# The last block of a fused attention and MoE kernel: one store per bank from two queues, and each bank copied by two engines

## The chip, the core and the metric

The kernel runs on one core of a Trainium2 chip. Its time is the device time of one execution in microseconds (us). The core has a matrix engine (TensorE, PE in the profile), a vector engine (VectorE, DVE), an activation engine (ScalarE, ACT), GpSimd (POOL) and a sync engine (SyncE, SP) that mostly issues transfers. Data are moved between device memory and the core's SBUF by 16 DMA engines; matrix products leave TensorE into eight banks of 128 partitions by 512 fp32 numbers (PSUM), from which ScalarE or VectorE copies them to SBUF.

## The reference

```python
batch, n_heads, seq, head_dim = (8, 8, 576, 64)
n_tokens, d_model, d_ff = (4608, 512, 2048)
...
out_d = sm_attn(q_d, k_d, v_d)          # on means of 4 tokens
out_up = np.repeat(out_d, factor, axis=2)
...
out_local = np.matmul(attn, v)          # band |i-j| < 4
return (out_up + out_local).astype(np.float32)
...
h = x @ w_in
P = a[0] + a[1] * h + a[2] * h2 + a[3] * h3
Q = 1.0 + np.abs(b[0]) * np.abs(h) + np.abs(b[1]) * h2
g = P / (Q + 1e-06)
return (g @ w_out).astype(np.float32)
```

The sum of a pooled and a local attention is the input x (4608 tokens by 512) of a two-layer network with a rational function between its layers. The result is 4608 rows of 512 fp32 numbers, 2 KB each, 9.44 MB in all.

## The kernel before, in words

Tokens go through the network in nine blocks of 512 (`block_plan`, L57). Block b of the first eight holds the first 512 tokens of batch b (`FULL`, L39). The ninth holds what is left, 64 tokens (`REST`) from each of the eight batches, so its output rows lie in eight pieces of the result, each 64 rows long, with 576 rows from the start of one to the start of the next. For the ninth block `blk.b` is None.

Each block takes 16 steps, one for each 128 of the 2048 hidden features (`steps`, L863). A step has a first-layer part (`h_part`, L899, matmul at L923), the rational function on ScalarE and VectorE (`middle`, L938) and a second-layer part (`o_part`, L974, matmul at L989). The second-layer part trails by two steps and adds into four banks, `ob[0]` to `ob[3]`, one for each 128 tokens of the block. After the last step `store(k)` (L1001) copies the four banks to SBUF and stores them.

The order on every engine comes from a planner (`Plan.run`, L118): each piece of work is put in with `add(engine, cost, function, reads, writes, due)`, and the planner starts what is ready by due time. What it returns is the order of issue; the waits between engines are then derived by the framework from what each instruction reads and writes.

In `store` the first eight blocks copy each bank with one ScalarE copy (L1012) and store it with one transfer of 128 rows from SP's queue (L1020). In the ninth, banks 0 and 2 are copied by ScalarE and banks 1 and 3 by VectorE (L1010), and each bank leaves in two transfers of 64 rows, since its 128 partitions hold the tails of two batches. These are eight transfers of 64 rows by 512 columns, all from SP. After them stands the end of the program: SP waits for every transfer's semaphore (L1247).

Of the kernel before, what the change touches and what calls it, by code (L numbers as in the profile page):

```python
# [17 lines left out]
B, H, S, D = 8, 8, 576, 64  # L18
NT = B * S
DM, DF = 512, 2048  # L20
P = 128
# [17 lines left out]
FULL = 512  # L39
# [17 lines left out]
def block_plan():  # L57
    plan = [Block([(b, 0, FULL)]) for b in range(B)]
    return plan + [Block([(b, FULL, REST) for b in range(B)])]
# [14 lines left out]
class Plan:  # L74
# [11 lines left out]
    def add(self, engine, dur, fn, reads=(), writes=(), due=None, lag=None, load=0.0, after=0.0):  # L86
        t = Task()
        t.engine, t.dur, t.fn, t.due, t.n = engine, dur, fn, due, len(self.tasks)
        t.load, t.after = load, after
        t.lag, t.preds, t.succs, t.late, t.start = lag, {}, [], 1e9, None  # L90
        rk = set().union(*(r.keys for r in reads)) if reads else set()
        wk = set().union(*(w.keys for w in writes)) if writes else set()
        t.uses = {k[1]: k in wk for k in rk | wk if k[0] == "P"}
        for k in rk | wk:
            w = self.writer.get(k)
            if w is not None:
                t.preds[w] = True
        for k in wk:
            for r in self.readers.get(k, ()):
                t.preds.setdefault(r, False)  # L100
            self.writer[k] = t
            self.readers[k] = []
        for k in rk - wk:
            self.readers[k].append(t) if k in self.readers else self.readers.__setitem__(k, [t])
        t.preds.pop(t, None)
        for p in t.preds:
            p.succs.append(t)
        self.tasks.append(t)
        return t
# [78 lines left out]
def attention_moe(  # L188
# [12 lines left out]
    nc = tc.nc  # L201
# [3 lines left out]
    add = plan.add  # L205
# [5 lines left out]
    def put(name, shape, dtype, at=None):  # L211
        nonlocal top
        offset = top if at is None else at
        n = 2 if dtype == BF16 else 4
        for d in shape[1:]:
            n *= d
        if at is None:
            top = -(-(offset + n) // 32) * 32
        ap = nc.alloc_sbuf_tensor_at(name, shape, dtype, offset=offset).ap()
        room = Room(ap, (("S", k) for k in range(offset // 32, -(-(offset + n) // 32))))  # L220
        room.at = offset
        room.size = n
        return room

    def part(room, ap, lo, n):

        r = Room(ap, (("S", k) for k in range((room.at + lo) // 32, -(-(room.at + lo + n) // 32))))
        r.at, r.size = room.at + lo, n
        return r

    def flat(t):
        return t.rearrange("p a b -> p (a b)")
# [5 lines left out]
    for name, parts in (("wl", low2), ("wh", high2)):  # L238
        for w in range(2):
            for f in range(0, NFC, 2):  # L240
                t = put(f"{name}{w}_{f}", [P, 2, NCC, P], F32R)
# [9 lines left out]
    xs, xsf = [], []  # L251
# [604 lines left out]
    blocks = block_plan()  # L856
# [9 lines left out]
    def due_h(n):  # L866
        m = blocks[0].nstep
        return H0 + H_FIRST * min(n, m) + H_STEP * max(0, n - m)
# [132 lines left out]
    def store(k):  # L1001
        blk = blocks[k]
        due = due_h(blk.first + blk.nstep + 2)
        for sub in range(blk.nsub):
            po = ob[sub]
            hi, osb = blk.x[0], xsf[blk.slot][0]
            room = part(hi, None, 4 * sub * DM, 4 * DM)
            osb = flat(osb.ap)[:, sub * DM : (sub + 1) * DM]
            if k == len(blocks) - 1 and sub % 2:
                add("DVE", 0.6, lambda osb=osb, po=po: nc.vector.tensor_copy(out=osb, in_=po.ap), (po,), (room,), due=due)  # L1010
            else:
                add("ACT", 0.49, lambda osb=osb, po=po: nc.scalar.copy(out=osb, in_=po.ap), (po,), (room,), due=due)  # L1012
            if blk.b is not None:
                rows = [(blk.b, sub * P, P)]
            else:
                rows = blk.rows[2 * sub : 2 * sub + 2]
            for i, (b, t, n) in enumerate(rows):
                add(
                    "SP", 0.7,
                    lambda osb=osb, b=b, t=t, n=n, i=i: nc.sync.dma_start(  # L1020
                        out=out[b * S + t : b * S + t + n, :], in_=osb[i * n : (i + 1) * n, :]
                    ),
                    (room,), (), due=due + 2,
                )


    order = sorted(((w, f) for w in range(2) for f in range(0, NFC, 2)), key=lambda c: c[1] / 2 + 1.5 * c[0])
# [69 lines left out]
    for n in range(NS + LAG):  # L1097
        if n < NS:
            k, s = steps[n]
            for f in range(blocks[k].fg):  # L1100
                h_part(n, f)
                if n < NAT:
                    if n % 2:
                        parts(0, n - 1, due_h(n - 1 + blocks[0].nstep) - 2.0)
                    if n == NAT - 1 and NAT < blocks[0].nstep:
                        split_x(0, due_h(NAT) - 3.0)
            if s == blocks[k].nstep - 1:

                if k + 1 < len(blocks):
                    split_x(k + 1)  # L1110
        o = n - LAG
        if o >= 0:
            k, s = steps[o]
            for f in range(blocks[k].fg):
                o_part(o, f)
            if s == blocks[k].nstep - 1:
                store(k)
                if blocks[k].b is not None and blocks[k].b + 2 < B:
                    attend(blocks[k].b + 2)

        if n < NS:
            middle(n)
# [21 lines left out]
    for t in pe:  # L1144
        at = idle_bank(t)
        n = int(WARM * (t.start - max(end, at[0])) / 0.107) if at else 0
# [105 lines left out]
```

## Time and profile before

| What | Value |
|---|---|
| median of 3 runs | 961.99 us (961.51 to 962.8) |
| the profiled execution | 961.83 us |
| its span, first to last instruction | 960.0 us |
| mean granted TensorE clock | 0.996 |
| TensorE busy | 939.1 us, 98% |
| VectorE / ScalarE busy | 843.4 us, 88% / 812.4 us, 85% |
| moved by the DMA engines | 89.26 MB |

The profile is of one execution. A row of the timeline reads: start and duration in us, engine, line, operation, output and input, shapes, number of instructions merged; in brackets what the engine waited for. SPq stands for instructions on SP that issue transfers. In the view of the DMA, a packet is one row of a transfer (or one write to a semaphore of 4 bytes, counted under 512 B), and a queue's share is the time that its packets took, of the time of all 16 DMA engines in the window.

### The profile page before, as it was taken

The page shows a single profiled execution, that of the slowest core. Times are in us where ns is not written, and L with a number is a line of the kernel's source. Part 1 is how long each engine was busy: PE and PEld are TensorE (multiplying, and loading weights), DVE is VectorE, ACT ScalarE, POOL GpSimd, SP SyncE. Part 2 cuts the span into 40 slices and gives each one's busy share as a digit, 9 for nine tenths or more (in the row PEclk, how much of TensorE's full clock was granted, in tenths as well). Part 3 has the DMA queues.
Part 4 walks back from the last instruction along what each step waited for, and adds up shares of the span by engine and source line. Part 5 has one row for each costly group of instructions (what it writes and reads, how often), then busy time and mean ns, then how long its engine had stood idle before and what let it go on. Part 6 is the DMA issues. An engine that isn't in the chain of part 4 may idle for free.

```text
span 960.0 us, 19318 instructions
## 1 busy us (share of the span) xinstructions
PE 939.1 (98%) x7184; PEld 738.1 (77%) x7184; DVE 843.4 (88%) x1430; ACT 812.4 (85%) x1992; POOL 121.1 (13%) x144
## 2 busy tenths in 40 slices
PE   7899999999999999999999999999999999999996
PEld 5565667878878788888878887878878888888885
DVE  7799999898889889798988898898979899988885
ACT  4799999999798888979797979888897977778674
POOL 1212022121102020212121210212021000000000
PEclk9999999999999999999999999999999999999999
DMA  9997477363333444343343423434332010001001
GB/s 298 279 326 194 105 191 175 84 123 84 72 99 62 108 69 110 63 107 58 94 93 76 89 58 110 74 93 77 102 57 51 1 45 1 1 1 45 1 0 45
DMA packets 44318, 89.26 MB, mean 93 GB/s; under 512 B 4992, under 2 KB 25856, under 8 KB 44224
## 3 DMA queue, kind: packets, MB, share of 16 engines
q1 hardware_dynamic: 25344, 63.52, 20.1%
q0 software_dynamic: 18880, 24.50, 17.7%
q8 instruction: 57, 0.93, 0.4%
q14 instruction: 37, 0.30, 0.1%
HBM read 74.37 MB, written 9.44 MB: 87 GB/s over the span
## 4 chain that ended last, share of the span: by engine, by line
PE 58%; ACT 20%; DVE 17%; issue 4%; DVEq 0%; POOL 0%; ACTq 0%; POOLq 0%
PE psum L989 26%; PE psum L923 25%; ACT m L936 6%; ACT el L739 4%; ACT epc L603 2%; DVE g L963 2%; DVE m L966 2%; DVE m L971 2%; ACT gb L936 2%; DVE g L972 2%; PE psum L911 2%; DVE m L951 1%; ACT epc L620 1%; DVE m L956 1%; DVE m L960 1%
## 5 line engine op out<-in xcount | busy, mean ns | idle before, releaser
L989 PE MATMUL psum<-wh,g 128*128 128x512 f32 x1152 | 392.2, 402 | 3.2 <-DVE g L972 1.4
L936 ACT ACTIVATE m<-psum,cf 128x512 f32<-128x512 f32 x288 | 216.0, 754 | 62.6 <-PE psum L923 54.8
L923 PE MATMUL psum<-xs,wh 128*128 128x512 f32 x1024 | 260.6, 394 | 0.0
L989 PEld LDWEIGHTS psum<-wh,g 128*128 128x128 f32 x1152 | 213.6, 188 | 55.7 <-DVE g L972 5.0
L989 PE MATMUL psum<-wl,g 128*128 128x512 f32 x576 | 224.3, 390 | 0.0
L923 PEld LDWEIGHTS psum<-xs,wh 128*128 128x128 f32 x1024 | 189.5, 188 | 42.2 <-issue 1.8
L963 DVE TENSOR_TENSOR g<-m,m 128x512 fp32r<-128x512 f32 x144 | 99.3, 690 | 65.7 <-ACT m L936 60.3
L923 PE MATMUL psum<-xs,wl 128*128 128x512 f32 x512 | 138.3, 392 | 0.0
L989 PEld LDWEIGHTS psum<-wl,g 128*128 128x128 f32 x576 | 108.2, 188 | 24.7 <-issue 2.2
L936 ACT ACTIVATE gb<-psum,cf 128x512 f32<-128x512 f32 x144 | 116.8, 811 | 10.4 <-PE psum L989 10.3
L936 ACT ACTIVATE gb<-m,cf 128x512 f32<-128x512 f32 x144 | 108.5, 754 | 19.6 <-DVE m L951 12.8
L474 POOL DMA_DIRECT2D pq<-in_qkp_dram x84 | 74.4, 929 | 383.5 <-DMA pq<-in_qkp_dram 305.0
L951 DVE SCALAR_TENSOR_TENSOR m<-m,cf,m 128x512 f32<-128x512 f32 x144 | 107.3, 745 | 6.9 <-ACT m L936 6.9
L923 PEld LDWEIGHTS psum<-xs,wl 128*128 128x128 f32 x512 | 95.4, 188 | 20.4 <-issue 0.6
L936 ACT ACTIVATE m<-gb 128x512 f32<-128x512 f32 x144 | 93.8, 651 | 19.4 <-DVE m L956 17.7
L960 DVE TENSOR_TENSOR m<-m,gb 128x512 f32<-128x512 f32 x144 | 99.0, 688 | 7.4
L966 DVE SCALAR_TENSOR_TENSOR m<-m,g 128x512 f32<-128x512 f32 x144 | 99.3, 690 | 3.4
L972 DVE TENSOR_TENSOR g<-m,m 128x512 fp32r<-128x512 f32 x144 | 98.7, 685 | 4.0
L971 DVE TENSOR_TENSOR m<-m,m 128x512 f32<-128x512 f32 x144 | 99.1, 688 | 2.6
L956 DVE TENSOR_TENSOR m<-m,m 128x512 f32<-128x512 f32 x144 | 98.5, 684 | 2.8 <-ACT m L936 2.8
L936 ACT ACTIVATE m<-psum 128x512 f32<-128x512 f32 x144 | 88.8, 617 | 0.0
L474 POOL DMA_DIRECT2D vpc<-in_vp_dram x42 | 34.9, 830 | 216.3 <-DMA vpc<-in_vp_dram 201.8
(78 smaller groups left out, 950.2 us busy)
## 6 DMA issues: line engine op xcount, KB each, us to landing
qk<-in_qk_dram SPq DMA_DIRECT2D x32, 590.0 KB, 3.9
pq<-in_qkp_dram POOLq DMA_DIRECT2D x84, 144.0 KB, 3.4
vw<-in_vw_dram SPq DMA_DIRECT2D x32, 320.0 KB, 4.0
out_dram<-xf SPq DMA_DIRECT2D x32, 256.0 KB, 2.4
vpc<-in_vp_dram POOLq DMA_DIRECT2D x42, 168.0 KB, 3.7
sx<-in_w_in_dram SPq DMA_DIRECT2D x5, 1024.0 KB, 12.2
sl<-in_w_out_dram SPq DMA_DIRECT2D x4, 1024.0 KB, 12.5
sx<-in_w_out_dram SPq DMA_DIRECT2D x4, 1024.0 KB, 6.5
```

What stands on the lines that cost most here:

```text
L474: lambda d=dst, x=x: nc.gpsimd.dma_start(out=d.ap, in_=x, accum_op=ALU.add),
L739: nc.scalar.activation(out=e[:, n], in_=e[:, n], func=AF.Exp, bias=nm[:, n : n + 1], scale=scale, accum_out=sm[:, n : n + 1],)
L923: nc.tensor.matmul(ph.ap[:, f * t : (f + 1) * t], lhsT=(high, low)[j][0][fc].ap[:, c, :], rhs=blk.x[i].ap[:, c, :] if blk.b is not None el ...
L936: add("ACT", cost, lambda: nc.scalar.activation(out=out_.ap, in_=in_, func=func, **kw), (room_in, cf, *more), (out_,))
L951: lambda: v.scalar_tensor_tensor(out=tb.ap, in0=tq.ap, scalar=b1, in1=tb.ap, op0=ALU.mult, op1=ALU.add),
L956: add("DVE", 0.61, lambda: v.tensor_tensor(out=ta.ap, in0=ta.ap, in1=tq.ap, op=ALU.mult), (ta, tq), (ta,))
L960: add("DVE", 0.61, lambda: v.tensor_tensor(out=ta.ap, in0=ta.ap, in1=u.ap, op=ALU.add), (ta, u), (ta,))
L963: add("DVE", 0.61, lambda: v.tensor_tensor(out=gh.ap, in0=ta.ap, in1=tq.ap, op=ALU.mult), (ta, tq), (gh,))
L966: lambda: v.scalar_tensor_tensor(out=tb.ap, in0=tb.ap, scalar=CONE, in1=gh.ap.bitcast(F32), op0=ALU.add, op1=ALU.mult),
L971: add("DVE", 0.61, lambda: v.tensor_tensor(out=tb.ap, in0=ta.ap, in1=tb.ap, op=ALU.subtract), (ta, tb), (tb,))
L972: add("DVE", 0.61, lambda: v.tensor_tensor(out=gl.ap, in0=tb.ap, in1=tq.ap, op=ALU.mult), (tb, tq), (gl,))
L989: nc.tensor.matmul(ob[sub].ap, lhsT=g[i].ap[:, f0 : f0 + P], rhs=flat((high, low)[j][1][fc].ap), start=(fc == 0 and m == 0), stop=(fc == N ...
```

## The change

Nothing changes but `store`, and in it only the ninth block (`blk.b is None`). Each bank is copied in two halves of 256 columns, the first by ScalarE and the second by VectorE. Each bank then leaves in one transfer: the source is 128 partitions by 512, the destination a view of the result with two batches, 64 rows and 512 columns. Banks 0 and 2 are issued from SP's queue, 1 and 3 from ScalarE's. The first eight blocks keep their copy and their transfer, written a little differently.

```diff
+            if blk.b is None:
+                lo, hi = (osb[:, i * DM // 2 : (i + 1) * DM // 2] for i in range(2))
+                plo, phi = (po.ap[:, i * DM // 2 : (i + 1) * DM // 2] for i in range(2))
+                rooms = [part(room, None, i * 2 * DM, 2 * DM) for i in range(2)]
+                add("ACT", 0.3, lambda o=lo, p=plo: nc.scalar.copy(out=o, in_=p), (po,), (rooms[0],), due=due)
+                add("DVE", 0.34, lambda o=hi, p=phi: nc.vector.tensor_copy(out=o, in_=p), (po,), (rooms[1],), due=due)
+                dst = out.rearrange("(b s) d -> b s d", s=S)[2 * sub : 2 * sub + 2, FULL:, :]
+                queue, engine = ("SP", nc.sync) if sub % 2 == 0 else ("ACT", nc.scalar)
+                add(
+                    queue, 0.7, lambda e=engine, d=dst, o=osb: e.dma_start(out=d, in_=o), (room,), (),
+                    due=due + 2 + sub,
+                )
+                continue
...
-            if k == len(blocks) - 1 and sub % 2:
-                add("DVE", 0.6, lambda osb=osb, po=po: nc.vector.tensor_copy(out=osb, in_=po.ap), (po,), (room,), due=due)
-            else:
-                add("ACT", 0.49, lambda osb=osb, po=po: nc.scalar.copy(out=osb, in_=po.ap), (po,), (room,), due=due)
...
-                rows = blk.rows[2 * sub : 2 * sub + 2]
-            for i, (b, t, n) in enumerate(rows):
```

The end of SP's queue before (xf_0_130 is the ninth block's SBUF buffer, xf_0_126 the eighth's; names with DMAHW are transfers' semaphores, and three line numbers were added above the end of the file):

```order
L1020 DMA out_dram<-xf_0_126 128x512 [waits DMAHW7_49,Activation_49]
L1020 DMA out_dram<-xf_0_130 64x512 [waits DMAHW0_49,Activation_49]
L1020 DMA out_dram<-xf_0_130 64x512 [waits DMAHW1_49]
L1020 DMA out_dram<-xf_0_130 64x512 [waits DMAHW2_49,DVE_49]
L1020 DMA out_dram<-xf_0_130 64x512 [waits DMAHW3_49]
L1020 DMA out_dram<-xf_0_130 64x512 [waits DMAHW4_49,Activation_49]
L1020 DMA out_dram<-xf_0_130 64x512 [waits DMAHW5_49]
L1020 DMA out_dram<-xf_0_130 64x512 [waits DMAHW6_49,DVE_49]
L1020 DMA out_dram<-xf_0_130 64x512 [waits DMAHW7_49]
L1247 UNCONDITIONAL_BRANCH
```

The same place in the changed kernel:

```order
L1025 DMA out_dram<-xf_0_126 128x512 [waits DMAHW5_49,Activation_49]
L1025 DMA out_dram<-xf_0_126 128x512 [waits DMAHW6_49,Activation_49]
L1025 DMA out_dram<-xf_0_126 128x512 [waits DMAHW7_49,Activation_49]
L1018 DMA out_dram<-xf_0_130 2x64x512 [waits DMAHW0_49,DVE_49]
L1018 DMA out_dram<-xf_0_130 2x64x512 [waits DMAHW2_49,DVE_49]
L1250 UNCONDITIONAL_BRANCH
```

Eight transfers of 64x512 became two here, written 2x64x512, and two more of the same form stand at the end of ScalarE's instructions, behind its four half copies. All four wait for VectorE.

The end of VectorE's instructions before:

```order
L966 SCALAR_TENSOR_TENSOR m_135<-m_135,g_139 128x512 [waits DVE_49]
L971 TENSOR_TENSOR m_135<-m_133,m_135 128x512 [waits DVE_49]
L972 TENSOR_TENSOR g_141<-m_135,m_137 128x512 [waits DVE_49,PE_49]
L1010 COPY xf_0_130<-psum 128x512 [waits DMAHW4_49,DMAHW3_49,DMAHW5_49,DMAHW2_49,DMAHW6_49,DMAHW1_49,DMAHW7_49,DMAHW0_49,PE_49]
L1010 COPY xf_0_130<-psum 128x512 [waits PE_49]
```

And after:

```order
L966 SCALAR_TENSOR_TENSOR m_135<-m_135,g_139 128x512 [waits DVE_49]
L971 TENSOR_TENSOR m_135<-m_133,m_135 128x512 [waits DVE_49]
L972 TENSOR_TENSOR g_141<-m_135,m_137 128x512 [waits DVE_49,PE_49]
L1014 COPY xf_0_130<-psum 128x256 [waits DMAHW4_49,DMAHW3_49,DMAHW5_49,DMAHW2_49,DMAHW6_49,DMAHW1_49,DMAHW7_49,DMAHW0_49,Activation_49]
L1014 COPY xf_0_130<-psum 128x256 [waits Activation_49] x3
```

VectorE's copies waited for TensorE before; now each waits for ScalarE, that is for the other half of the same bank. The instructions of TensorE and GpSimd, and those of all engines ahead of the ninth block's copies, stand in the order that they had.

More of the change, by code (lines that the diff above doesn't have):

```diff
@@ L1005, in store @@
             po = ob[sub]
-            hi, osb = blk.x[0], xsf[blk.slot][0]
-            room = part(hi, None, 4 * sub * DM, 4 * DM)
+            xhi, osb = blk.x[0], xsf[blk.slot][0]
+            room = part(xhi, None, 4 * sub * DM, 4 * DM)
             osb = flat(osb.ap)[:, sub * DM : (sub + 1) * DM]
-            if k == len(blocks) - 1 and sub % 2:
-                add("DVE", 0.6, lambda osb=osb, po=po: nc.vector.tensor_copy(out=osb, in_=po.ap), (po,), (room,), due=due)
-            else:
-                add("ACT", 0.49, lambda osb=osb, po=po: nc.scalar.copy(out=osb, in_=po.ap), (po,), (room,), due=due)
@@ L1013, in store @@
-            if blk.b is not None:
-                rows = [(blk.b, sub * P, P)]
-            else:
-                rows = blk.rows[2 * sub : 2 * sub + 2]
-            for i, (b, t, n) in enumerate(rows):
-                add(
[L1019 to L1023, printed above, removed]
-                )
+            if blk.b is None:
[6 more added lines that the diff above has]
+                queue, engine = ("SP", nc.sync) if sub % 2 == 0 else ("ACT", nc.scalar)
+                add(
+                    queue, 0.7, lambda e=engine, d=dst, o=osb: e.dma_start(out=d, in_=o), (room,), (),
+                    due=due + 2 + sub,
+                )
+                continue
@@ L1027, in attention_moe @@
+            add("ACT", 0.49, lambda osb=osb, po=po: nc.scalar.copy(out=osb, in_=po.ap), (po,), (room,), due=due)
+            add(
+                "SP", 0.7,
+                lambda osb=osb, b=blk.b, t=sub * P: nc.sync.dma_start(out=out[b * S + t : b * S + t + P, :], in_=osb),
+                (room,), (), due=due + 2,
+            )
     order = sorted(((w, f) for w in range(2) for f in range(0, NFC, 2)), key=lambda c: c[1] / 2 + 1.5 * c[0])
```

## The prediction

> **What bounds the kernel now.** I read the page first, then the chain of work that ended last, then the end of the timeline, then the DMA view of that end. The page's head and its first part say what the whole is worth:
>
> ```profile
> span 960.0 us, 19318 instructions
> PE 939.1 (98%) x7184; PEld 738.1 (77%) x7184; DVE 843.4 (88%) x1430; ACT 812.4 (85%) x1992; POOL 121.1 (13%) x144
> ```
>
> TensorE is busy for 98% of the span, and the order of its instructions is the same after the change. So what the change can move is the stretch behind the last matmul. The profiled execution took 961.83 us, 1.83 more than its span and 0.16 below the median of the three runs (961.99). I add this 1.83 to every span below. A measurement of this kernel can tell about 0.2%, 1.92 us, from no change.
>
> The chain in its last 12 us, start and duration first, and the timeline of the same place:
>
> ```profile
> 951.04 0.72 PE psum L989 x2
> 951.76 0.02 issue
> 951.78 0.69 DVE xf L1010
> 952.47 0.60 DVEq L1247
> ```
> ```profile
> 951.04 1.17 PE L989 MATMUL psum<-wh,g 128*128 128x512 f32 x4
> 951.54 1.07 ACT L1012 COPY xf<-psum 128x512 f32<-128x512 f32 x2 [3.62 <-PE psum L989]
> 951.78 1.29 DVE L1010 COPY xf<-psum 128x512 f32<-128x512 f32 x2 [0.89 <-PE psum L989]
> 952.16 5.18 SPq L1020 DMA_DIRECT2D out_dram<-xf  x8
> ```
>
> The chain stops at about 953.1, but the span ends at 960.0: what lies between is in no row of the chain, it is the eight stores. SP issues them from 952.16 to 957.34, one each 0.65 us, 128 KB each. The DMA view of the last 8 us (40 slices of 0.2 us) shows the data:
>
> ```profile
> DMA  0000003998997988279779959989979880000000
> GB/s 0 0 0 0 0 0 82 225 205 205 215 195 174 256 195 184 72 195 246 174 205 205 236 144 225 205 205 215 205 164 266 184 184 21 0 0 0 0 0 0
> DMA packets 641, 1.06 MB, mean 132 GB/s; under 512 B 128, under 2 KB 128, under 8 KB 640
> q1 hardware_dynamic: 640, 1.05, 57.0%
> out_dram<-xf SPq DMA_DIRECT2D x8, 128.0 KB, 2.3
> ```
>
> Data begin within the seventh slice, at about 953.3, 1.15 us behind the first issue. They end at about 958.6, 1.4 us before the end of the span. In between the engines are nearly full at about 205 GB/s. So the end of this kernel is 952.16 + 1.15 + 5.3 + 1.4 = 960.0: an issue, a start, 1.05 MB of rows, and a closing.
>
> **The rows' price.** 57.0% of 16 engines over 8 us is 73.0 engine-us for 512 rows of 2 KB: 142 ns for a row on its engine. The same bytes cost less in the stores of the eighth block, four of 128 rows (window 870.7 to 874.7, slices of 0.1 us):
>
> ```profile
> DMA  0000000028999999999999999999999999994000
> DMA packets 576, 1.05 MB, mean 262 GB/s; under 512 B 64, under 2 KB 64, under 8 KB 576
> q1 hardware_dynamic: 576, 1.05, 70.4%
> out_dram<-xf SPq DMA_DIRECT2D x4, 256.0 KB, 2.3
> ```
> ```profile
> 870.75 1.81 SPq L1020 DMA_DIRECT2D out_dram<-xf  x4
> ```
>
> 70.4% of 16 engines over 4 us is 45.1 engine-us for 512 rows, 88 ns a row. First data come 0.85 us behind the issue here, and the last 3.6 us behind it. A store of 128 partitions is thus worth having, if it keeps 16 engines busy.
>
> **Does it keep them?** The packets under 512 B are the writes to semaphores that close a transfer: 128 for eight stores, 64 for four, 16 each. So both forms, 64 rows and 128, are dealt to all 16 engines, 4 rows or 8 for each. In both, source and destination have the same leading count, a multiple of 16. The changed stores are the first without it: 128 partitions on one side, 2 pieces of 64 rows on the other (2x64x512 in the order). If a transfer is cut once, at the leading count of both sides, only a cut in two fits; if it is dealt row by row, 16 engines get 8 rows each as before. The issue times speak for the single cut:
>
> ```profile
> L360 SPq DMA_DIRECT2D sx<-in_w_in_dram x5: 378/379/912, 4.6 to 117.1; - x5
> L458 SPq DMA_DIRECT2D qk<-in_qk_dram x32: 327/339/503, 0.7 to 692.2; - x32
> L1020 SPq DMA_DIRECT2D out_dram<-xf x40: 332/348/594, 164.9 to 956.7; - x40
> ```
>
> A weight load of 256 runs takes 379 ns to issue (median, the middle number), a load of 128 rows 339: 128 more runs cost 40 ns. The issuer does not walk rows. I take the cut in two as the likeliest. The Trainium skill states this as a rule (DMA: Bandwidth & Descriptors, "Why a DMA increments its semaphore by 16 and not by 1"): the number of engines is the largest up to 16 that divides the slowest dimension of both sides, and below 16 it takes the lowest-numbered ones. By that rule the four stores would share two engines; the 16 closing writes agree with it for 64 and 128 rows, and no run here yet shows a leading 2.
>
> **The change part by part.**
>
> Half copies. Their rows in this kernel are of other sizes:
>
> ```profile
> L796 ACT COPY et<-psum 128x128 f32<-128x128 f32 x32 | 7.4, 306 | 0.0
> L1012 ACT COPY xf<-psum 128x512 f32<-128x512 f32 x2 | 1.1, 590 | 3.6 <-PE psum L989 3.6
> L1010 DVE COPY xf<-psum 128x512 f32<-128x512 f32 x2 | 1.3, 686 | 0.9 <-PE psum L989 0.9
> L670 DVE TENSOR_TENSOR xf<-psum,up 128x64 f32<-128x64 f32 x32 | 6.0, 215 | 0.0
> 936.41 0.63 ACT L936 ACTIVATE m<-gb 128x512 f32<-128x512 f32 x1
> 937.08 0.69 DVE L963 TENSOR_TENSOR g<-m,m 128x512 fp32r<-128x512 f32 x1 [0.44 <-ACT m L936]
> ```
>
> A ScalarE half lies between 306 and 590 ns; by the columns (256 between 128 and 512) 0.40 us. A VectorE half lies between 215 and 686 ns; 0.42 us by the columns. In the changed order VectorE's half waits for ScalarE's of the same bank, so the two do not run side by side but behind each other; the handoff from ScalarE to VectorE is 0.04 us (937.04 to 937.08). ScalarE's first copy starts at 951.54 as now. Its bank is ready for the store at 951.54 + 0.40 + 0.04 + 0.42 = 952.40. Now it is ready at 951.54 + 0.59 = 952.13, and the issue follows 0.03 later. So the first store is issued at 952.43, 0.27 us later than now (0.0 to 0.65 with the ends of the copies). Behind that wait stand only VectorE's three other halves, one each 0.42 us. The last bank is ready at 953.66, and the last store's issue, now at 956.7, comes at about 953.7 on ScalarE, which has nothing else left.
>
> Stores. Four issues in place of eight, from two queues. ScalarE has issued no transfer in this program, so its price is bounded by SP's rows, 0.33 to 0.59 us, and above by a start that is late by some us. It lies beside the rows of SP's two stores, which keep the two engines busy for 11 us; without that cover it would cost its own length.
>
> Rows. Cut in two, each store puts 64 rows on each of two engines, and if all four go to the same two, each has 256 rows: 45.1 engine-us over 2 engines, 22.5 us. Bounds: the early loads run all engines at
>
> ```profile
> DMA packets 291, 1.01 MB, mean 402 GB/s; under 512 B 28, under 2 KB 56, under 8 KB 291
> ```
>
> (window 60.0 to 62.5), 25.1 GB/s for one engine, by which 1.05 MB on two takes 20.9 us. At the price of the present 64-row stores, 73.0 engine-us, it is 36.5 us. I take 22.5, since the rows come from all 128 partitions as in the eighth block's stores, at the same size.
>
> The sum: 952.43 + 1.15 (start, from the last stores) + 22.5 + 1.4 (closing) = 977.5 us of span, 979.3 us of time: 17.5 us, 1.8%, slower. With the bounds 977.7 to 993.3. Nothing hides any of it: the other engines have ended by 954.
>
> **Rivals.**
>
> *Sixteen engines.* If the dealing goes by rows, the four stores keep all engines. First issue 952.43, 0.3 for the later first data (1.15 against 0.85), 3.6 from first issue to last data as in the eighth block, 1.4 to close: span 957.7, time 959.6, 2.2 us and 0.23% faster. For it speaks that every transfer looked at has 16 closings; against it, that none of them had sides that disagree, and that issuing 256 runs costs hardly more than 128. It decides from the first slice of the last stores: 16 engines busy or two. It ends as no change if the last store is issued later than 953.7 by over 0.3 us, as a slow first issue on ScalarE's queue would make it.
>
> *Two pairs.* If SP's stores go to one pair and ScalarE's to another, each engine has 128 rows, 11.3 us: span 952.43 + 1.15 + 11.3 + 1.4 = 966.3, time 968.1. All transfers that SP and GpSimd issue here use all 16 engines, so the trace shows nothing of a pair. The Trainium skill holds against it that queues of several engines run on the same 16 DMA engines, and that a second one saves only time of issue (the same page, "Issuing engines are not separate DMA queues"). By that the sum stays at 22.5 us of rows; no transfer here came from ScalarE, so no run shows it.
>
> *The halves beside each other.* That the change does not do what it says is already in the sum: the order shows one half behind the other. If it cost nothing, the sum would fall by 0.27 us, in any of the cases.
>
> **How the numbers follow.** The cut in two on one pair has 0.82: a single cut explains the flat issue times and all the closings seen. Two pairs have 0.03. Sixteen engines have 0.15, of which 0.09 are faster by over 0.2% and 0.06 within it, since 2.2 us is just beyond 1.92 and a late last store takes it back. Slower by over 0.2% is thus 0.85. The time is that of the likeliest, 979.3. The range leaves out the 0.18 of the others and about 0.02 of the likeliest. Below, 25.1 GB/s for an engine gives 977.7, and 0.27 less if the halves cost nothing; the last 2.4 us down to 975 are for two engines that go faster alone than beside fourteen others (1.05 MB on two in 18.5 us, 28.3 GB/s each). Above, 126 ns a row, two thirds of the way from 88 to 142, gives 32.2 us of rows: 989.
>
> **What would show it.** In the changed profile the DMA share behind 953.5 should be near 2 of 16, 12 to 13%, at some 45 GB/s, for about 22 us; the four stores should have 8 closing writes together in place of 64; the first store should be issued at 952.4 and VectorE's halves each start behind ScalarE's. A share near 100% for 3 us means sixteen engines and a time near 959.6; about 25% for 11 us means two pairs. A time off these three would mean that a row has another price on two engines, or that the start or the closing grew.

## The result, and the profile after

| | before | changed |
|---|---|---|
| median | 961.99 us (5 runs, 960.38 to 965.11) | 979.68 us (5 runs, 978.28 to 980.17) |
| profiled execution / its span | 961.83 / 960.0 us | 978.28 / 976.4 us |
| first copy of the last block to the end of the span ("tail") | 8.5 us | 25.7 us |

The ratio is 1.0177 (95% interval 1.0156 to 1.0198): 1.8% slower, where 979.3 us was forecast.

The tail is the measure that the rest uses: what lies ahead of it is the same program in all kernels but those that reorder the last block's tokens, and differs from run to run by some us. It starts when ScalarE begins the last block's first copy. The page of the changed kernel and the end of its timeline:

```profile
span 976.4 us, 19316 instructions
PE 938.6 (96%) x7184; PEld 737.9 (76%) x7184; DVE 843.9 (86%) x1432; ACT 811.9 (83%) x1994; POOL 120.9 (12%) x144
```
```profile
950.73 1.20 ACT L1013 COPY xf<-psum 128x256 f32<-128x256 f32 x4 [3.62 <-PE psum L989]
951.14 1.42 DVE L1014 COPY xf<-psum 128x256 f32<-128x256 f32 x4 [1.05 <-ACT xf L1013]
951.59 1.29 SPq L1018 DMA_DIRECT2D out_dram<-xf  x2
951.92 1.71 ACTq L1018 DMA_DIRECT2D out_dram<-xf  x2
```

TensorE's busy time is what it was (939.1 then, 938.6 now), and all four stores are issued by 953.6, where eight took until 957.3. Then nothing runs but the DMA. Its view from 952.8 to 974.9, in 40 slices of 0.55 us:

```profile
DMA  1121011111111111111111111111111111111110
GB/s 22 15 37 30 30 52 52 52 52 52 52 48 48 52 52 52 52 52 52 52 52 48 48 52 52 52 52 52 52 52 52 48 48 52 52 52 52 52 52 37
DMA packets 521, 1.06 MB, mean 48 GB/s; under 512 B 8, under 2 KB 8, under 8 KB 520
q1 hardware_dynamic: 260, 0.52, 6.9%
q10 hardware_dynamic: 260, 0.52, 6.1%
```

Where the digits stood at 8 and 9 for 5 us, they stand at 1 for 22. The shares of the two queues (q1 is SP's, q10 ScalarE's) add to 13.0% of 16 engines, which is 2.08 engines; the rate is 52 GB/s in place of 205. And eight packets under 512 B close four stores, two each, in place of 16 each.

### The profile page after: what moved, and what is told of

Same layout as the page of the kernel before. It is cut to its first block, busy times and chain, and to the rows that moved or that the text cites. A ratio compares the mean times of both kernels' runs of the same rounds, so it can differ in the third digit from the quotient of the medians.

```text
span 976.4 us, 19316 instructions
## 1 busy us (share of the span) xinstructions
PE 938.6 (96%) x7184; PEld 737.9 (76%) x7184; DVE 843.9 (86%) x1432; ACT 811.9 (83%) x1994; POOL 120.9 (12%) x144
## 3 DMA queue, kind: packets, MB, share of 16 engines
q0 software_dynamic: 18880, 24.50, 17.5%
## 4 chain that ended last, share of the span: by engine, by line
PE 56%; ACT 20%; DVE 17%; issue 5%; DVEq 0%; POOL 0%; ACTq 0%; POOLq 0%
PE psum L989 24%; PE psum L923 24%; ACT m L936 6%; ACT el L739 4%; ACT epc L603 3%; DVE g L963 2%; DVE m L966 2%; ACT gb L936 2%; DVE m L971 2%; DVE g L972 2%; ACT epc L620 2%; DVE m L956 2%; DVE m L951 2%; ACT el L577 2%; DVE m L960 1%
```

## The experiments

Eight kernels, four on one chip and four on another, each beside runs of the kernel before. Medians of the kernel before beside them were 962.20 and 962.21 us. Order: first what of the change costs, then whether the leading count sets it, then what is left of the change without it.

**The form of the store alone.** The kernel before, with this in place of its last eight stores:

```diff
+            if blk.b is None:
+                dst = out.rearrange("(b s) d -> b s d", s=S)[2 * sub : 2 * sub + 2, FULL:, :]
+                add("SP", 0.7, lambda osb=osb, dst=dst: nc.sync.dma_start(out=dst, in_=osb), (room,), (), due=due + 2)
+                continue
```

> The kernel before with one edit: each bank of the last block leaves in one store written 2x64x512; copies as before, all four stores from SP. I compare tails, from the start of ScalarE's first copy of the last block to the end of the span: 8.5 us before, 25.7 in the changed kernel. Theory (engines): a store is cut once, at the leading count of both sides, so these four run on two engines whichever queue issues them: rows for about 22 us, tail 25.4, time 979. Rival (queue): the loss comes from ScalarE's queue, whose first data came 4.5 us behind its issue: with SP alone the tail is 7 to 8.5 and the time 960 to 962. Rival (pieces): a destination in two pieces is slow for each row, on whatever engines: 979 too, so this run does not tell it from the first.

Measured: 978.24 us, ratio 1.0171 (1.0155 to 1.0186), tail 25.2. Timeline of the end, and the DMA from 951 to 976:

```profile
951.16 1.07 ACT L1012 COPY xf<-psum 128x512 f32<-128x512 f32 x2 [3.62 <-PE psum L989]
951.40 1.29 DVE L1010 COPY xf<-psum 128x512 f32<-128x512 f32 x2 [0.89 <-PE psum L989]
951.77 9.97 SPq L1019 DMA_DIRECT2D out_dram<-xf  x4
```
```profile
DMA packets 521, 1.06 MB, mean 42 GB/s; under 512 B 8, under 2 KB 8, under 8 KB 520
q1 hardware_dynamic: 520, 1.05, 11.4%
```

With whole copies and one queue the loss is there: 16.7 us of the 17.2 by which the tail grew. ScalarE's queue and the half copies have next to no part in it. The rival that a destination in two pieces is slow is open after this run; the leading counts below settle it.

**Two stores of 64 rows again.** The changed kernel with its store alone undone:

```diff
-                add(
-                    queue, 0.7, lambda e=engine, d=dst, o=osb: e.dma_start(out=d, in_=o), (room,), (),
-                    due=due + 2 + sub,
-                )
+                for i in range(2):
+                    add(
+                        queue, 0.7,
+                        lambda e=engine, d=dst[i], o=osb[i * REST : (i + 1) * REST, :]: e.dma_start(out=d, in_=o),
+                        (room,), (), due=due + 2 + sub,
+                    )
```

> The changed kernel with one edit undone: each bank leaves in two stores of 64 rows again, banks 0 and 2 from SP, 1 and 3 from ScalarE, the copies in halves. Theory (engines): leading counts of 64 on both sides, all 16 engines, 16 closing writes for each store: 2.1 us to the first data, at most 5.3 of rows, 1.5 to close, tail 8.0 to 9.0, time 961 to 963; shorter if two queues read both halves of the partitions at once. Rival (queue): ScalarE's queue keeps most of the loss, tail over 15, time over 968.

Measured: 961.44 us, ratio 0.9994 (0.9985 to 1.0004), tail 7.7, a little under the expected 8.0 to 9.0. The DMA from 952 to 960:

```profile
DMA packets 642, 1.07 MB, mean 133 GB/s; under 512 B 128, under 2 KB 128, under 8 KB 640
q10 hardware_dynamic: 320, 0.52, 26.3%
q1 hardware_dynamic: 320, 0.52, 20.3%
```

128 closing writes for eight stores, 16 each, and the loss is gone with both queues and both halves in place. 46.6% of 16 engines over 8 us is 59.6 engine-us, where one queue's eight stores took 73.0 before: with two queues the same 64-row stores have cheaper rows, and why was not tried. The time cannot be told from that of the kernel before.

**A leading count of 8, and of 64.** Both reorder the tokens of the last block so that one store of 128 partitions can be written with another leading count. The first-layer matmul reads its columns in that order; the output is the same. For 8 (each bank 16 tokens of all eight batches):

```diff
-                        rhs=blk.x[i].ap[:, c, :] if blk.b is not None else tails(blk.x[i], c).ap,
+                        rhs=blk.x[i].ap[:, c, :] if blk.b is not None else tails(blk.x[i], c).ap.rearrange("p b (s t) -> p s b t", t=P // B),
...
-                dst = out.rearrange("(b s) d -> b s d", s=S)[2 * sub : 2 * sub + 2, FULL:, :]
+                dst = out.rearrange("(b s) d -> b s d", s=S)[:, FULL + sub * P // B : FULL + (sub + 1) * P // B, :]
```

For 64 (the two batches of a bank alternate from partition to partition):

```diff
+                        rhs=blk.x[i].ap[:, c, :] if blk.b is not None else tails(blk.x[i], c).ap.rearrange("p (s b) t -> p s t b", b=2),
...
+                dst = out.rearrange("(b s) d -> s b d", s=S)[FULL:, 2 * sub : 2 * sub + 2, :]
```

> The changed kernel with the last block's tokens in another order: the first-layer matmul of that block reads its columns so that a bank holds 16 tokens of each of the eight batches, and its one store is written 8x16x512, from the same two queues. Output unchanged. Theory (engines): 8 closing writes for each store, rows on eight engines: 45.1 engine-us over 8 is 5.6 us, tail 2.1 + 5.6 + 1.5 = 9.2, time 962.7 (up to 964 if ScalarE's first data are as late as 4.5 us). Rival (pieces): eight pieces in place of two are as slow or slower: tail 25 or more, time 979 or more.

> The changed kernel with the last block's tokens in another order: the first-layer matmul of that block reads its columns so that the two batches of a bank alternate from partition to partition, and its one store is written 64x2x512, from the same two queues. Output unchanged. Theory (engines): 64 and 128 leave 16 engines and 16 closing writes, rows for 2.8 us, tail 2.1 + 2.8 + 1.5 = 6.4, time 959.9; if ScalarE's first data come 4.5 us behind its issue here too, tail 8.7 and time 962.2. Rival (pieces): 64 pieces of two rows are as slow as two pieces of 64: tail 25, time 979. Should the strided read of the columns cost TensorE time, it shows in the matmuls of the last block, 0.4 us each now.

Measured with 8: 968.18 us, ratio 1.0064 (1.0051 to 1.0078), tail 11.1. With 64: 959.76 us, ratio 0.9975 (0.9962 to 0.9987), tail 7.1. The DMA of the first from 954 to 965, and of the second from 949 to 957:

```profile
DMA packets 545, 1.06 MB, mean 96 GB/s; under 512 B 32, under 2 KB 32, under 8 KB 544
q1 hardware_dynamic: 272, 0.52, 16.5%
q10 hardware_dynamic: 272, 0.52, 13.3%
```
```profile
DMA packets 577, 1.06 MB, mean 132 GB/s; under 512 B 64, under 2 KB 64, under 8 KB 576
q10 hardware_dynamic: 288, 0.52, 17.7%
q1 hardware_dynamic: 288, 0.52, 17.7%
```

Closing writes for each store: 2, 8 and 16 with leading counts of 2, 8 and 64. Tails: 25.7, 11.1 and 7.1. The destination has 2, 8 and 64 pieces for a store, so the rival that pieces are slow would have gone the other way; it is out. The Trainium skill's rule (DMA: Bandwidth & Descriptors, "Why a DMA increments its semaphore by 16 and not by 1"), by which the largest number up to 16 that divides both sides' slowest dimension sets the engines, agrees with all of these.

The size for 8 was off: 11.1 against 9.2, and 968.2 against 962.7. 29.8% of 16 engines over 11 us is 52.4 engine-us, 6.6 us on eight engines where 5.6 were counted, and the engines were not full from the first row on. The other 3.6 us lie ahead of the tail, 3.1 of them in a longer last block (below). With 64 the tail missed too, 7.1 against 6.4; the time still came out near the 959.9 that was expected, since the last block ahead of the tail was 1.6 us shorter, which was not forecast.

**The halves alone.** The kernel before, with the half copies and nothing else (the two `add` lines of the change, for `blk.b is None`):

> The kernel before with one edit: each bank of the last block is copied in halves by ScalarE and VectorE, as in the changed kernel; eight stores of 64 rows from SP as before. By the prediction's step the first store is issued 0.27 us later (0.24 in the changed kernel's trace: 0.86 against 0.61 us behind the first copy's start) and the stores go on as before: tail 8.7 against 8.5, time within 0.2% of before. Rival: the halves give the later banks sooner and the tail shortens by some tenths.

Measured: one time, 964.12 us, tail 8.7 against 8.5. The end of its timeline:

```profile
953.55 1.20 ACT L1013 COPY xf<-psum 128x256 f32<-128x256 f32 x4 [3.62 <-PE psum L989]
953.96 1.42 DVE L1014 COPY xf<-psum 128x256 f32<-128x256 f32 x4 [1.06 <-ACT xf L1013]
954.41 5.18 SPq L1026 DMA_DIRECT2D out_dram<-xf  x8
```

The first store goes out 0.86 us behind the first copy's start where it was 0.61, and the eight stores take 5.18 us to issue as before: the halves make the tail 0.24 us longer. The whole time is one run and 1.9 us above the median beside it, 0.20%; its first copy starts 2.0 us later than in the profile of before, so that lies ahead of the tail. The rival, that the halves shorten the end, is out for this form of store.

**ScalarE's queue alone.** The changed kernel with one edit:

```diff
-                queue, engine = ("SP", nc.sync) if sub % 2 == 0 else ("ACT", nc.scalar)
+                queue, engine = "ACT", nc.scalar
```

> The changed kernel with all four 2x64x512 stores issued from ScalarE's queue. In the changed kernel ScalarE's first data came 4.5 us behind its issue, in the runs with leading counts of 8 and 64 it was 3.1 and 1.7. Theory (rows ahead): they wait behind the rows that SP had already put on the same engines; alone, ScalarE's first data come 1.2 to 1.7 us behind its first issue, and the tail is 25 to 26 as before, since the two engines are the same. Rival (slow queue): ScalarE's queue is slow to start with stores of this form: first data 4 us or more behind the issue, tail 28 or more. If each queue had engines of its own, two queues would have halved the rows already; they did not.

Measured: one time, 980.22 us, tail 26.2. Timeline, and the DMA from 952 to 978 in slices of 0.65 us:

```profile
953.03 10.03 ACTq L1018 DMA_DIRECT2D out_dram<-xf  x4
```
```profile
DMA  0000111111111111111111111111111111111000
GB/s 0 0 0 19 25 32 25 38 41 54 50 54 50 50 50 50 50 50 54 54 50 50 50 50 47 50 50 54 54 50 50 50 50 50 50 54 50 16 0 13
DMA packets 522, 1.06 MB, mean 41 GB/s; under 512 B 8, under 2 KB 8, under 8 KB 520
q10 hardware_dynamic: 520, 1.05, 11.0%
```

First data come between 954.0 and 954.6 (the GB/s row has its first 19 there), 1.3 us behind the issue by the packets themselves. So the queue is not slow to start when nothing is ahead of it. Nor is its first issue the reason, which took 1.14 us in both kernels. In the changed kernel its rows came behind SP's on the same two engines; there the DMA from 951.9 to 956.4, and from 956.4 to 962, reads

```profile
DMA packets 55, 0.12 MB, mean 26 GB/s; under 512 B 0, under 2 KB 0, under 8 KB 54
q1 hardware_dynamic: 54, 0.11, 10.3%
```
```profile
DMA packets 140, 0.29 MB, mean 51 GB/s; under 512 B 0, under 2 KB 0, under 8 KB 140
q1 hardware_dynamic: 70, 0.14, 6.6%
q10 hardware_dynamic: 70, 0.14, 6.6%
```

SP's rows are alone until 956.4, 4.5 us behind ScalarE's issue at 951.92, and then the rows of the two queues alternate, 70 of each. Why the turns did not begin sooner was not tried.

**One store per bank that keeps 16 engines, without the halves.** The kernel before with the interleaved order and the store 64x2x512, from SP alone, and then with banks 1 and 3 from ScalarE's queue:

> The kernel before with the interleaved order of the last block's tokens and one store 64x2x512 for each bank, all from SP, whole copies as before. Sixteen engines: first issue 0.61 us behind the first copy, first data 1.9, issues some 0.7 apart, last data at about 4.8, tail 6.7 to 7.0 against 8.5 before and 7.1 with halves and two queues; time 959.5 (ratio to before 0.997 to 0.998). The last block's first-layer matmuls should read 379 ns again in place of 389, if the order of the columns is what shortened them. Rival: four issues from one queue are the limit and the tail stays over 7.5.

> The same as the run before it, but banks 1 and 3 are issued from ScalarE's queue. If the issues of one queue limit it, two queues shorten the tail to 6.5, where 2.8 us of rows on 16 engines are the limit; if the rows are the limit already, both tails are equal within 0.2 us. Time 959 to 960.

Measured: 958.77 us, ratio 0.9966 (0.9955 to 0.9978), tail 6.9, and 959.14 us, ratio 0.9967 (0.9954 to 0.9980), tail 6.7. Timeline and DMA (950 to 957) of the first, then of the second:

```profile
950.38 1.07 ACT L1012 COPY xf<-psum 128x512 f32<-128x512 f32 x2 [3.62 <-PE psum L989]
951.00 2.90 SPq L1019 DMA_DIRECT2D out_dram<-xf  x4
```
```profile
DMA  0000000000000799999982699999993000000000
DMA packets 577, 1.06 MB, mean 151 GB/s; under 512 B 64, under 2 KB 64, under 8 KB 576
```
```profile
950.51 1.07 ACT L1012 COPY xf<-psum 128x512 f32<-128x512 f32 x2 [3.63 <-PE psum L989]
951.12 1.31 SPq L1020 DMA_DIRECT2D out_dram<-xf  x2
951.46 1.31 ACTq L1020 DMA_DIRECT2D out_dram<-xf  x2
```
```profile
DMA  0000000000000299999999999999971000000000
```

With one queue the engines run nearly dry once, at about 953.7, between the rows of two stores; with two they do not, and the tail is 0.25 us shorter, between the 6.5 and the equal tails that were expected. In their times the two kernels are equal. Both beat the kernel before, by 0.3%, and the changed kernel by some 2%. Of the 3.4 and 3.1 us by which their medians lie below that of the kernel before, 1.6 and 1.8 are the tail's; the last block ahead of it is 1.6 us shorter (below), which leaves at most 0.3 us to differences between runs.

## Why the prediction was right, step by step

- **What bounds the end.** Right: nothing covers the stores, and the whole of the loss is in the tail. It grew from 8.5 to 25.7 us, 17.2, where 17.5 were forecast.
- **The half copies.** 0.40 and 0.42 us were taken between bounds of 306 and 590, and of 215 and 686 ns; 0.39 and 0.41 were measured. VectorE's half stands behind ScalarE's, as the order showed (idle 1.05 us until ScalarE ended). The first store was issued 0.86 us behind the first copy; the sum had 0.89. VectorE's halves followed each other every 0.33 us and not every 0.42, so the last bank was ready 1.8 us behind the first copy, where the sum had 2.1; nothing hung on it.
- **The cut in two.** Right, and the step on which all hung. It was argued from issue times that hardly grow with the rows and from 16 closings each, neither of which could show a leading 2. The run with the form alone, and the counts of 2, 8 and 64, show it.
- **The same two engines.** Right: two queues share 2.08 engines, and one queue alone takes as long (25.2 and 26.2 us).
- **The rows.** 22.5 us was taken, from the eighth block's stores; the view of the DMA has 22. By the queues' shares, the measure that gave the sum its 88 ns, a row took 90 ns (13.0% of 16 engines over 22.1 us, for 512 rows). The stretch was not even: the first five slices were slower, and at the 52 GB/s behind them a row left each engine every 79 ns. In the upper bound, 126 ns is 0.70 of the way from 88 to 142; two thirds would be 124, and 988.5 in place of 989.
- **Start and closing.** 1.15 and 1.4 us were taken from the old stores; 1.25 and 1.6 were measured. (The last packet of the old stores ends at 958.75, so their closing was nearer 1.3.) The sum of the tail was 25.9 against 25.7. The profiled execution came out 1.0 us under the forecast because its first copy also started 0.8 us earlier than in the profile of before.
- **ScalarE's issue.** Its price was bounded by SP's rows, 0.33 to 0.59 us, and taken as one that the other stores cover. The two issues took 1.14 and 0.53 us, the first outside that bound, and the first data came 4.5 us behind it; both were covered. Alone the queue started in 1.3 us, so it is not slow in itself; SP's rows were ahead of it.
- **The rival of sixteen engines.** Its price was 959.6. Made to happen by the order of tokens, with the changed kernel's copies and queues, it gave 959.76, but not by the sum that was forecast: its tail was 7.1, where that sum (957.7 less 951.54) had 6.2, and a last block that was 1.6 us shorter made up for it. That the time agrees is luck.

## What to carry to other kernels

Fewer and larger stores are a gain only if the written form keeps the engines: read the leading count of both sides of a transfer, and count its closing writes in the profile. At the end of a program, where nothing hides a transfer, two engines in place of sixteen cost 17 us for 1 MB. Where the destination's pieces force a small leading count, either keep one store for each piece, or reorder the work so that the long dimension leads.

## What the runs showed of the hardware that was not expected

**The order of columns changes the matmul.** The last block's first-layer matmuls in the window 885 to 940, of the kernel before (runs of 64 columns), with the leading count of 8 (runs of 16), and with one store from SP and the interleaved order (single columns, in turn from two batches whose columns lie 1 KB apart):

```profile
L923 PE MATMUL psum<-xs,wh 128*128 128x512 f32 x80 | 19.8, 389 | 0.0
```
```profile
L923 PE MATMUL psum<-xs,wh 128*128 128x512 f32 x80 | 20.7, 401 | 0.0
```
```profile
L923 PE MATMUL psum<-xs,wh 128*128 128x512 f32 x81 | 19.3, 379 | 0.0
```

These times overlap, so they cannot be added up: below, eight matmuls of 389 ns take 1.98 us together. What the order costs is read from the whole last block, from its first first-layer matmul to the first copy. Timelines of the same three kernels (the first copy is at 951.54 in the first and at 950.38 in the third, shown above):

```profile
859.29 1.98 PE L923 MATMUL psum<-xs,wh 128*128 128x512 f32 x8
```
```profile
859.45 2.07 PE L923 MATMUL psum<-xs,wh 128*128 128x512 f32 x8
954.80 1.20 ACT L1013 COPY xf<-psum 128x256 f32<-128x256 f32 x4 [3.63 <-PE psum L989]
```
```profile
859.73 1.89 PE L923 MATMUL psum<-xs,wh 128*128 128x512 f32 x8
```

The block takes 92.25 us with runs of 64, 95.35 with runs of 16 and 90.65 with single columns: 3.1 us more and 1.6 less. All six kernels with runs of 64 agree on this length within 0.01 us, and so do the three with single columns, while the start of the block moves from 858.5 to 861.3 between runs. Shorter runs are slower in one case and faster in the other, so their length alone does not decide. In the kernel with runs of 16 the second-layer matmuls are longer too (392 and 394 ns against 389). Why the order matters was not tried.

**An issue can take microseconds.** With four 2x64x512 stores in one queue the third and fourth issue took long; of the run from ScalarE's queue alone:

```profile
L1018 ACTq DMA_DIRECT2D out_dram<-xf x4: 527/2290/4797, 953.0 to 958.3; - x4
```

The longest took 4.8 us, where an issue of this form took 0.53 at the least. The third ended at 958.22 and the fourth at 963.05. The DMA from 953 to each of these two times:

```profile
DMA packets 67, 0.14 MB, mean 26 GB/s; under 512 B 0, under 2 KB 0, under 8 KB 67
```
```profile
DMA packets 189, 0.38 MB, mean 38 GB/s; under 512 B 2, under 2 KB 2, under 8 KB 189
```

Without the two closing writes that is 67 and 187 rows begun, of 384 and 512 issued by then: each issue ended with some 320 rows still to come (317 and 325). In the run with the form alone, from SP's queue, it was 318 and 326. In the changed kernel, where no queue had more than 256 rows, no issue took over 1.14 us. A queue that holds some 160 rows for each of the two engines, and an issue that waits for room, would fit; no run varied the number of rows, so this is not shown. An issue that waits holds what stands behind it on its engine: the fourth issue here started at 958.26, when the third was done.
